# An attention-and-MLP kernel on one core: exponential tiles in any free cells, four more VectorE units in each of two late quads, another start, value fills in quarters

## The chip, the core and the metric

The kernel runs on one core of one Trainium2 chip. The metric is the device time of one execution in microseconds (us). Executions of one kernel mostly agree within 0.3%. With one core there is no second die to compare with, so every run here counts as an ordinary (fast) one.

Two lengths have to be kept apart. The *time* is what the device reports for the execution. The *span* is what the trace shows, from the first to the last instruction.

A ratio of two kernels is the mean time of one kernel's fast runs over the mean of the other's in the same rounds. It is therefore not quite the ratio of the medians that are quoted beside it. The interval behind a ratio is a 95% interval. "Same" means within 2%.

## The reference

Attention over 32 heads and a bilinear MLP read the same `x`; a sigmoid gate mixes them. S = 2048, D = 512, a head has 16 columns, F = 1376; all inputs are bf16.

```
g = sigmoid((x * gate_w).sum(-1, keepdims=True))
q, k, v = split_heads(x @ wqkv)                  # 32 heads of 16
p = softmax(q @ k^T * 16**-0.5)                  # 32 x 2048 x 2048
a = concat_heads(p @ v) @ wo
b = ((x @ w_gate) * (x @ w_up)) @ w_down
out = g * a + (1 - g) * b
```

The softmax needs 32 x 2048 x 2048 exponentials, 134 million. As 128 x 512 tiles these are 2048 tiles. Everything in this kernel is arranged around them.

## The kernel before

The work is cut into 32 *quads*: 4 heads (index `j`) times 512 queries. A quad has 16 key tiles `kt` times 4 heads, so 64 score tiles. For each `kt`, three of the four go to ScalarE, which takes two or three neighbouring tiles in one exponential. The fourth goes to VectorE as a *unit*: a first conversion of the scores to int16 gives the bits of an approximate exponential, and three copies with shifted bits (`k` = 1, 2, 3), made for two tiles at a time by VectorE or GpSimd, refine it. The products with the values then weight the four variants by values that were scaled beforehand (`VD`, and `VE` for extra units). So ScalarE has 48 tiles in a quad and VectorE 16.

The results live in *cells*: 512 columns of bf16 in the buffer `PT` (54 cells) and, as long as or as soon as they are idle, in buffers of other data (`wv`, `hT`, `wd`). A cell is free again when the products that read it are done. All other work of TensorE (projections of q, k, v, the MLP, the output projection) is cut into *fills*, packs of matmuls that are slipped in between scores and products.

The order of instructions is not written down. A *builder* (Python in the kernel file that runs when the program is built) plays through the execution with its own estimates of durations and puts each instruction at the first place where it sees its inputs ready. The positions of the fills carry a fixed pseudo-random jitter, chosen by `SEED`. A small edit can therefore move thousands of instructions.

The parts that the change touches (cuts marked with `...`). First the constants, the first loads, the choice of units:

```
NMAIN = 54                       # cells in PT
RA = 24
HB = []                          # head groups with extra VectorE units: none
XU = {0: 2, 5: 3, 10: 0, 15: 1}
...
d_wq[0] = load("act", wq[:, :, 0:128], wcol(0, 128), ...)
d_wk[0] = load("act", wk[:, :, 0:128], wcol(D, D + 128), ...)
d_wv[0] = load("act", wv[:, :, 0:256], wcol(2 * D, 2 * D + 256), ...)
...                              # then 12 transposing loads of x on "sp"
def xd(m, kt, j):                # is this tile an extra unit of VectorE?
    return (m % NQ) // 2 in HB and XU.get(kt) == j
```

The search for free cells: `alloc` gives ScalarE the first cell of `n` consecutive free cells from one set of areas, and VectorE and GpSimd an aligned pair from another set.

```
segs = [(0, RA, 9999), (C_V, 4, 9999), (C_H, FT, EH), (C_D, 5, ED)]     # ScalarE
prs = [(RA, NMAIN, 9999), (C_D + 5, C_D + FT, ED)]                      # pairs

def alloc(n, t, pair=False, keep=0):
    if pair:
        for i in sorted(pair_starts(), reverse=True):
            if is_free(i, t) and is_free(i + 1, t):
                ...
                return i
        return None
    ...                          # tightest run of at least n free cells in a row
    return None if best is None else best[1]
```

The evacuation of the first keys, the value fill in two packs of 16 matmuls, and the copies of the first transposed x:

```
def evac(bk, last):                                    # in f_k, the keys
    if b == ch == 0:
        ev_k[b, ch] = add("act", [last], lambda a: a.activation(dst, bk.ap, ACT.Copy), ...)
        return
...
for t2 in range(2):                                    # in f_v, the values
    def mk(bk, t=t, t2=t2):
        for kt in range(KD):                           # KD = 4
            for q in range(4):
                r = e.matmul(bk.ap[...], xT[:, kt, ...], wv[:, kt, ...], ...)
    packs.append((mk, 0.5, "c"))
...
ex = now("dve", [o_last], lambda v: v.tensor_copy(xT[:, kt, 0:512], src), 0.42)
```

The exponential itself, and a pair copy on VectorE:

```
c = alloc(n, t)
k = _Task("act", [sc] + old,
    lambda a: a.activation(cell_ap(c, n), src, ACT.Exp, scale=LN2 / 128.0), ...)
...
fn = lambda v: v.tensor_single_scalar(cell_ap(c, n, I16), cell_ap(pr["cell"], n, I16), 32.0 * k, ALU.add)
```

The softmax here doesn't subtract the row's maximum and nothing guards it: scores larger than these inputs give would overflow.

## Time and profile before

| | before |
|---|---|
| time, median of 3 runs | 721.21 us (721.11 to 721.33) |
| span of the profiled execution | 719.0 us |
| ScalarE, TensorE, VectorE, GpSimd busy | 98%, 95%, 88%, 57% |
| first exponential starts | 9.43 us |
| exponentials (with the gate's small ones) | 698.8 us |
| visible waits of ScalarE among them | 1.9 us |
| last exponential to the end of the span (tail) | 8.9 us |

The last four rows add up to the span. They are read from the records of ScalarE: the third is the end of the last exponential, less the start of the first, less the waits.

The head of the profile page and the chain of waits of the kernel before. The first line has, for each engine, its busy time, its share of the span and its instructions (PE is TensorE, PEld its weight loads, DVE VectorE, ACT ScalarE, POOL GpSimd). The second has the share of each engine in the chain of work that ended last, followed back from the end:

```profile
...
PE 686.3 (95%) x9079; PEld 188.6 (26%) x9079; DVE 633.8 (88%) x1209; ACT 702.8 (98%) x688; POOL 411.6 (57%) x433
...
ACT 95%; PE 3%; DMA 1%; DVE 1%; ACTq 0%; issue 0%; DVEq 0%
...
```

95% of the chain is ScalarE. The table of windows agrees: below, after the stretch, come its length and then the busy time of each engine in it, with the instructions in brackets, the TensorE clock that was granted, and the DMA share.

```profile
...
core 0: us, PE busy (x) PEld busy (x) DVE busy (x) ACT busy (x) POOL busy (x), PEclk, DMA share, GB/s
...
100.00:200.00 100.00, 95.84 (x1268) 25.80 (x1265) 91.40 (x175) 100.00 (x98) 61.88 (x66) 1.00 0.10 29
...
600.00:700.00 100.00, 95.77 (x1240) 25.37 (x1241) 88.91 (x169) 100.00 (x97) 53.26 (x51) 1.00 0.05 15
...
```

ScalarE is busy 100.00 of 100.00 us in both stretches, and so in the others between. TensorE and VectorE stand at 89 to 96. Such a "100%" has to be read with care. The groups of exponentials by form give the mean recorded duration as the last number before the second bar:

```profile
...
L1598 ACT ACTIVATE PT<-psS 128x1024 bf16<-128x1024 f32 x326 | 359.7, 1269 | 0.0
L1598 ACT ACTIVATE PT<-psS 128x1536 bf16<-128x1536 f32 x147 | 247.4, 1695 | 0.0
...
```

An exponential of two tiles is recorded with 1269 ns, but in a steady stretch the next one *starts* 0.917 us after it (median; three tiles: 1.343 us). So neighbours overlap by about 0.35 us, and a wait shorter than that does not show. What is visible is the list of waits of ScalarE (line, what released it: us in total, times, longest):

```profile
...
ACT KE L572 <- PE psS L543: 3.9, 1, 3.9
ACT L363 <- issue: 2.9, 1, 2.9
ACT hT L1598 <- PE psS L477: 2.4, 4, 1.0
ACT oraw L1808 <- PE psS L543: 1.7, 1, 1.7
```

The two lines that read `KE` and `L363` are before the first exponential, `oraw` is after the last one. In between only the line `hT L1598` remains: four waits, 2.4 us, for scores. One of them (0.49 us) is the wait for the very first scores; the other three come to 1.91 us, and all lie before 28 us. Two of them are long: 0.67 us at 15.3 us and 1.02 us at 26.5 us. The timeline before the second one (start, duration, engine, line, operation; in brackets the idle time before it):

```profile
...
24.75 0.37 PE L477 MATMUL psS<-QM,KE 32*128 32x512 bf16 x2
...
25.06 0.83 PE L543 MATMUL psS<-xT,wk 128*32 128x512 bf16 x12
...
25.71 1.05 PE L627 MATMUL psS<-wv,xT 128*32 128x256 bf16 x32
...
26.59 0.61 PE L627 MATMUL psX<-wv,xT 128*32 128x256 bf16 x16
...
27.13 0.39 PE L477 MATMUL psS<-QM,KE 32*128 32x512 bf16 x2
...
27.56 1.02 ACT L1598 ACTIVATE hT<-psS 128x1024 bf16<-128x1024 f32 x1 [1.02 <-PE psS L477]
...
```

The last scores before the wait began at 24.75 us; then TensorE did 12 matmuls of keys, 32 and 16 of values, and only at 27.13 us the next scores.

And the way to the first exponential:

```profile
...
1.80 0.53 ACTq L316 DMA_DIRECT2D wk<-in_A_wqkv_dram  x1
...
7.24 1.05 PE L543 MATMUL psS<-xT,wk 128*32 128x512 bf16 x16 [0.38 <-DMA wk<-in_A_wqkv_dram]
8.34 0.60 ACT L572 ACTIVATE KE<-psS 128x512 bf16<-128x512 f32 x1 [3.93 <-PE psS L543]
...
9.00 0.39 PE L477 MATMUL psS<-QM,KE 32*128 32x512 bf16 x3
...
9.43 3.28 ACT L1598 ACTIVATE hT<-psS 128x1024 bf16<-128x1024 f32 x3 [0.49 <-PE psS L477]
...
```

The first key weights are issued at 1.80 us as the third load on the ScalarE queue (after half of the first x and the query weights) and land at 7.20 us, the key matmuls wait for them until 7.24 us, the copy of the keys takes 0.60 us, and the first exponential starts at 9.43 us.

### The profile page before, as it was taken

Reading aid. Unit: us, or ns where it says so; the run is one execution under the profiler, and the core shown is the slowest. Engines: PE = TensorE matmul, PEld = TensorE weight load, DVE = VectorE, ACT = ScalarE, POOL = GpSimd, SP = SyncE. Lnnn points to the kernel's source line nnn. Section 1 sums busy time; section 2 is a strip of 40 time slices with the busy share of each in tenths; the row PEclk is TensorE's granted clock in tenths of the full one; section 3 lists DMA queues with packets and bytes.
Section 4 is the critical chain, followed back from the end, with each engine's and each line's share of the span. In section 5 each row is a group of like instructions: output and inputs, shape, how many; then the busy total and the mean of one; then the engine's idle time right before and its main releaser. Section 6 shows DMA issues by size and latency. Waiting matters only on the chain.

```text
span 719.0 us, 21551 instructions
## 1 busy us (share of the span) xinstructions
PE 686.3 (95%) x9079; PEld 188.6 (26%) x9079; DVE 633.8 (88%) x1209; ACT 702.8 (98%) x688; POOL 411.6 (57%) x433
## 2 busy tenths in 40 slices
PE   8999999999999999999999999999999999999996
PEld 3323232222222222222222222222222222222222
DVE  5888999998998889889998888989888999898887
ACT  5999999999999999999999999999999999999996
POOL 3777756665665455565455564665555655555541
PEclk9999999999999999999999999999999999999999
DMA  7800001000300000100000011000000010000001
GB/s 140 255 4 32 6 17 21 18 16 8 96 21 16 18 16 19 39 18 21 17 18 12 17 34 34 17 6 17 21 17 16 14 36 24 17 16 21 10 13 46
DMA packets 33054, 21.66 MB, mean 30 GB/s; under 512 B 20380, under 2 KB 27964, under 8 KB 32960
## 3 DMA queue, kind: packets, MB, share of 16 engines
q1 hardware_dynamic: 31104, 19.51, 9.4%
q8 instruction: 72, 1.18, 0.7%
q10 hardware_dynamic: 1856, 0.79, 0.5%
q14 instruction: 22, 0.18, 0.1%
HBM read 15.12 MB, written 2.36 MB: 24 GB/s over the span
## 4 chain that ended last, share of the span: by engine, by line
ACT 95%; PE 3%; DMA 1%; DVE 1%; ACTq 0%; issue 0%; DVEq 0%
ACT PT L1598 69%; ACT wv L1598 16%; ACT hT L1598 5%; ACT wd L1598 4%; PE psS L543 1%; DMA wk<-in_A_wqkv_dram 1%; PE psO L1150 1%; PE psS L477 0%; PE psS L627 0%; PE psX L627 0%; DVE wk L851 0%; PE psX L477 0%; DVE wd L1029 0%; PE psX L543 0%; ACTq L316 0%
## 5 line engine op out<-in xcount | busy, mean ns | idle before, releaser
L1598 ACT ACTIVATE PT<-psS 128x1024 bf16<-128x1024 f32 (+1 forms) x473 | 540.0, 1402 | 0.0
L1088 POOL TENSOR_SCALAR PT<-PT 128x1024 int16<-128x1024 int16 x312 | 322.2, 1043 | 250.8 <-DVE PT L1085 129.2
L1029 DVE TENSOR_SCALAR PT<-psS 128x512 int16<-128x512 f32 x441 | 300.0, 686 | 47.4 <-PE psS L477 40.6
L477 PE MATMUL psS<-QM,KE 32*128 32x512 bf16 x1981 | 263.5, 375 | 22.7 <-ACT PT L1598 8.6
L1150 PE MATMUL psO<-PT,VS 128*18 128x512 bf16 x1597 | 220.9, 381 | 0.3 <-DVE oraw L1179 0.2
L1150 PE MATMUL psO<-PT,VD 128*18 128x512 bf16 x1400 | 204.5, 381 | 0.2
L1085 DVE TENSOR_SCALAR PT<-PT 128x1024 int16<-128x1024 int16 x380 | 155.8, 450 | 4.6 <-PE psO L1150 1.4
L1598 ACT ACTIVATE wv<-psS 128x1024 bf16<-128x1024 f32 (+1 forms) x120 | 154.7, 1335 | 0.0
L971 PEld LDWEIGHTS <-KE 32*128 32x128 bf16 x2048 | 63.1, 90 | 274.7 <-issue 273.4
L1150 PEld LDWEIGHTS psO<-PT,VS 128*18 128x18 bf16 x1597 | 51.5, 88 | 63.8 <-issue 38.1
L1150 PE MATMUL psO<-wv,VS 128*18 128x512 bf16 x257 | 63.1, 381 | 0.1
L1150 PEld LDWEIGHTS psO<-PT,VD 128*18 128x18 bf16 x1400 | 47.5, 88 | 42.1 <-issue 27.4
L543 PE MATMUL psX<-wd,hT 128*32 128x512 bf16 (+1 forms) x704 | 55.9, 385 | 0.0
L543 PE MATMUL psX<-xT,wu 128*32 128x512 bf16 x688 | 55.8, 384 | 0.0
L1598 ACT ACTIVATE hT<-psS 128x1024 bf16<-128x1024 f32 (+1 forms) x49 | 53.4, 1274 | 2.4 <-PE psS L477 2.4
L543 PE MATMUL psX<-xT,wg 128*32 128x512 bf16 x688 | 55.2, 384 | 0.0
L1029 DVE TENSOR_SCALAR PT<-psX 128x512 int16<-128x512 f32 x63 | 43.4, 688 | 8.6 <-PE psS L477 8.2
L1598 ACT ACTIVATE wd<-psS 128x1024 bf16<-128x1024 f32 (+1 forms) x34 | 42.5, 1340 | 0.0
L1088 POOL TENSOR_SCALAR wd<-PT 128x1024 int16<-128x1024 int16 x26 | 27.0, 1043 | 9.3 <-DVE wd L1085 4.2
L790 DVE TENSOR_TENSOR hT<-psX,usb 128x512 bf16<-128x512 f32 (+1 forms) x44 | 30.0, 683 | 2.1 <-PE psX L543 1.9
L758 DVE CAST usb<-psX 128x512 bf16<-128x512 f32 (+1 forms) x44 | 30.0, 681 | 2.0 <-PE psO L1150 0.9
L1211 POOL TENSOR_TENSOR OT<-oraw,rb 128x512 bf16<-128x512 f32 x16 | 20.4, 1273 | 13.7 <-DVE PT L1085 13.7
(94 smaller groups left out, 453.9 us busy)
## 6 DMA issues: line engine op xcount, KB each, us to landing
rb<-rscr SPq DMA_DIRECT2D x31, 256.0 KB
out_dram<-ost SPq DMA_DIRECT2D x12, 128.0 KB, 1.7
wu<-in_B_w_up_dram SPq DMA_DIRECT2D x1, 1376.0 KB, 8.0
wg<-in_B_w_gate_dram SPq DMA_DIRECT2D x1, 1376.0 KB, 11.6
wd<-in_B_w_down_dram SPq DMA_DIRECT2D x1, 1280.0 KB, 6.2
OT<-OX SPq DMA_DIRECT2D x60, 16.0 KB, 1.8
wo<-in_A_wo_dram SPq DMA_DIRECT2D x1, 512.0 KB, 12.3
out_dram<-wk SPq DMA_DIRECT2D x4, 128.0 KB, 1.7
```

What stands on the lines that cost most here:

```text
L477: return e.add_instruction(mybir.InstMatmult(name=nc.get_next_instruction_name(), engine=mybir.EngineType.PE, ins=[e.lower_ap(rhs), e.lowe ...
L543: return e.matmul(out_ap[32 * q : 32 * q + w, :], lhs[:, 32 * q : 32 * q + w], rhs, start=s0, stop=s1, tile_position=(0, 32 * q), skip_gro ...
L758: lambda v: v.tensor_copy(usb[0:w, n % 2, :], bk.ap[0:w, :]),
L790: lambda v: v.tensor_tensor(hT[0:w, f, :], bk.ap[0:w, :], usb[0:w, n % 2, :], ALU.mult),
L971: r = e.ldweights(w, tile_position=pos)
L1029: lambda v: v.tensor_scalar(cell_ap(pr["cell"] + i, 1, mybir.dt.int16), bk.ap, CB, 0.0, ALU.add, ALU.max),
L1085: fn = lambda v: v.tensor_single_scalar(cell_ap(c, n, I16), cell_ap(pr["cell"], n, I16), 32.0 * k, ALU.add)
L1088: fn = lambda g: g.tensor_scalar(cell_ap(c, n, I16), cell_ap(pr["cell"], n, I16), 32.0 * k, 1.0, ALU.add, ALU.mult)
L1150: r = e.matmul(psO[32 * j : 32 * j + VW, :], pv_stationary(m, kt, j, k), cell_ap(cell, 1), start=s0, stop=s1, tile_position=(0, 32 * j), s ...
L1211: lambda e: e.tensor_tensor(dst, oraw[:, s, :], rb[:, s, :], ALU.mult),
L1598: lambda a: a.activation(cell_ap(c, n), src, ACT.Exp, scale=LN2 / 128.0),
```

## The change

Its intent, in the words of the change: exponential tiles may lie in any free cells, by strided writes; VectorE takes more units in two late quads; a shorter way to the first scores; value fills in quarters. The diff is 650 lines; this is its core.

```diff
-    HB = []
-    XU = {0: 2, 5: 3, 10: 0, 15: 1}
+    HBQ = [24, 30]                       # quads with extra units
+    HB = sorted({(m % NQ) // 2 for m in HBQ})
+    XU = {1: 3, 4: 2, 7: 1, 10: 0}
...
-            return (m % NQ) // 2 in HB and XU.get(kt) == j
+            return m in HBQ and XU.get(kt) == j
```
```diff
-        d_wk[0] = load("act", wk[:, :, 0:128], wcol(D, D + 128), "dwk0", 0.5, 3.6)
+        d_wk[0] = load("sp", wk[:, :, 0:128], wcol(D, D + 128), "dwk0", 0.5, 4.4)
...
-                    ev_k[b, ch] = add("act", ..., a.activation(dst, bk.ap, ACT.Copy), ...)
+                    ev_k[0, 0, 0] = add("act", ..., a.activation(dst[:, 0:128], bk.ap[:, 0:128], ACT.Copy), ...)
+                    ev_k[b, ch] = add("act", ..., a.activation(dst[:, 128:512], bk.ap[:, 128:512], ACT.Copy), ...)
...
-            ex = now("dve", ..., v.tensor_copy(xT[:, kt, 0:512], src), 0.42)
+            if kt % 2:
+                ex = now("act", ..., a.activation(xT[:, kt, 0:512], src, ACT.Copy), ...)
+            else:
+                ex = now("dve", ..., v.tensor_copy(xT[:, kt, 0:512], src), 0.35)
```
```diff
-        def cell_ap(c, n, dt=None):
+        def cell_ap(c, dt=None):             # c: a tuple of cells
...
+            dims = [[1, 512]]
+            if len(c) > 1:
+                d = c[1] - c[0]
+                dims = [[1, 512 * len(c)]] if d == 1 else [[512 * d, len(c)], [1, 512]]
...
-        segs = [(0, RA, 9999), (C_V, 4, 9999), (C_H, FT, EH), (C_D, 5, ED)]
-        prs = [(RA, NMAIN, 9999), (C_D + 5, C_D + FT, ED)]
+        groups = [(C_H, FT, EH), (C_D, FT, ED), (C_V, 4, 9999), (0, NMAIN, 9999)]
...
+            for f in fr:                     # the free cells of one buffer
...                                           # n in a row, if there are,
+                if n == 2:
+                    return (f[0], f[1])      # else any two,
...                                           # or three or four with equal steps
```
```diff
-                def mk(bk, t=t, t2=t2):
-                        for kt in range(KD):
+                for kh in range(2):
+                    def mk(bk, t=t, t2=t2, kh=kh):
+                            for kt in (2 * kh, 2 * kh + 1):
...
-                packs.append((mk, 0.5, "c"))
+                    packs.append((mk, 0.23, "c"))
...
-        SEED = 2
+        SEED = 3
```

The cuts hold changes of bookkeeping: fills of the two quads are spread thinner, a VectorE copy may take two pairs at once, the builder's estimates of durations are adjusted, the order of the first fills is written differently.

What the built programs show: ScalarE goes from 1536 tiles in 676 exponentials (490 of two tiles, 185 of three, one of one) to 1528 tiles in 674 (494 of two, of which 12 are strided, and 180 of three, of which 2 are strided). VectorE goes from 512 to 520 first conversions. The copies of pairs stay at 424 instructions on VectorE (19 with a strided output, 2 of four tiles) and go from 344 to 354 on GpSimd (9 with a strided output). So strides are rare: 14 of 674 exponentials. Before, ScalarE looked for cells in one set of areas and VectorE and GpSimd in another; now all three may take any free cell.

## The prediction

> **What bounds the kernel now.** ScalarE. The table of windows has it always busy from 100 to 700 us. The chain of waits is 95% ScalarE, nearly all exponentials. The list of waits gives it only 2.4 us of waiting for scores (four times, all before 28 us). The span is 719.0 us; the time 721.21 us.
>
> From the ScalarE timeline, start to start, an exponential of two tiles (1024 columns) takes 0.917 us, one of three (1536) 1.343 us: 0.426 us a tile and 0.064 us an instruction. The Trainium skill, page "ScalarE: Activation LUTs", section "What ACT_TABLE_LOAD costs", says one element per cycle and lane at 1.2 GHz, 0.833 ns a column; the trace agrees (0.832). Its fixed part less overlap, 93 ns, exceeds the 64 seen; I use the trace.
>
> The span is: head 9.43 us (start of the first exponential), 698.3 us of exponentials plus 0.46 for the gate, 1.9 us of later score starvation, and a tail of 8.9 us (710.1 to 719.0).
>
> **What the change does**
>
> 1. VectorE takes 4 more units in each of quads 24 and 30. ScalarE goes from 1536 tiles in 676 instructions (490 of two, 185 of three, one of one) to 1528 in 674 (494 and 180), read from the built programs. Estimate: 4×0.917 − 5×1.343 − 0.49 = −3.5 us, all critical. VectorE gets 8 first conversions (0.69 us each recorded) and there are 12 more pair copies, of which GpSimd (57% busy) takes 10. VectorE is about 89% busy, but gets fewer projection fills in those quads; I expect it to fit.
> 2. Free cells with strides. 14 exponentials, 19 VectorE and 9 GpSimd copies become strided. Each inner run stays 512 contiguous elements, so I expect contiguous durations. ScalarE never waited visibly for a cell: direct gain nil; it supports step 1.
> 3. Shorter head. The first key weights were issued at 1.80 us and arrived at 7.20, the last wait before the first keys. They now go on the sync queue ahead of the transposing loads; I estimate arrival about 1 us earlier. Two of four x copies go to ScalarE (idle then), and the key copy (0.60 us) is split so that 128 columns (about 0.3 us) release the first scores. First exponential at about 8.5 us: −0.9 us, critical. No extra table load: a copy ran there before with one load.
> 4. Value fills in quarters let scores slip in between (a 16-matmul half takes 0.62 us of TensorE). Of 1.9 us starvation about 1.0 should remain: −0.9 us.
> 5. Tail unchanged, 8.9 us ± 0.4.
>
> Sum −5.3 us. I take back 0.5 us for new short waits of ScalarE, as everything is reordered: −4.8 us.
>
> **Prediction: 716.4 us, 8 in 10 between 714.0 and 719.0.** Chances: faster by over 2% 0.01, within 2% 0.975, slower by over 2% 0.015.
>
> **What would show it.** Step 1: exponentials 3.5 us less in total, start-to-start times still 0.917 and 1.343, no ScalarE waiting late. Step 2: strided forms with the mean of contiguous ones. Step 3: first exponential near 8.5 us. Step 4: ScalarE waiting for scores about 1 us after the first exponential. Step 5: last exponential to end 8.9 us.
>
> **What would make it wrong.** VectorE or TensorE (95% busy) cannot keep up in quads 24 and 30, so ScalarE waits there; strided writes slow ScalarE; the early key weights delay the x transposes, so later keys and values come late and early starvation grows; the last product waits for copies, lengthening the tail.

## The result and the profile after

| | time, median | runs |
|---|---|---|
| before | 721.24 us | 721.11 to 721.33, n = 4 |
| after | 715.65 us | 714.12 to 715.74, n = 4 |

The ratio is 0.9918 [0.9901, 0.9935]: 0.8% faster, "same" by the 2% rule. The profiled execution is the 714.12 us one; its span is 712.5 us. The head of its page and its chain:

```profile
...
PE 683.8 (96%) x9103; PEld 187.7 (26%) x9103; DVE 641.4 (90%) x1215; ACT 700.3 (98%) x689; POOL 428.4 (60%) x467
...
ACT 65%; PE 28%; DVE 4%; issue 2%; POOL 0%; DVEq 0%; ACTq 0%
...
```

The chain is now 65% ScalarE and 28% TensorE, where it was 95% ScalarE. It would be wrong to read this as a change of the bound. The windows and the waits, which decide it, say the opposite:

```profile
...
100.00:200.00 100.00, 95.53 (x1301) 26.68 (x1297) 93.39 (x175) 99.90 (x97) 66.10 (x74) 1.00 0.11 30
...
600.00:700.00 100.00, 96.62 (x1236) 24.74 (x1228) 91.70 (x177) 100.00 (x100) 58.06 (x56) 1.00 0.05 16
...
```

```profile
...
ACT L365 <- issue: 2.4, 1, 2.4
ACT oraw L1870 <- PE psS L551: 1.7, 1, 1.7
ACT KE L581 <- PE psS L551: 1.5, 1, 1.5
ACT xT L1774 <- PE psS L1764: 1.3, 1, 1.3
```

ScalarE is busy 99.90 and 100.00 of 100.00 us, and its list has four lines which are all before the first exponential or (`oraw`) after the last: no wait of any length worth a line remains among the exponentials. A likely reason for the new shares of the chain, argued and not tested: when ScalarE's next input and its own previous instruction are ready at nearly the same moment, the chain may go either way, and TensorE (96% busy) runs close to ScalarE.

The exponentials by form:

```profile
...
L1656 ACT ACTIVATE PT<-psS 128x1024 bf16<-128x1024 f32 x397 | 420.9, 1259 | 0.2
L1656 ACT ACTIVATE PT<-psS 128x1536 bf16<-128x1536 f32 x172 | 284.8, 1679 | 0.0
...
```

There are more lines with `PT` and fewer with other buffers, because cells are now searched in another order. The means (1259 and 1679 ns) are not longer. Start to start, an exponential of two tiles takes 0.916 us (0.917 before), one of three 1.331 us (1.343). Of the 12 strided ones of two tiles nine take 0.904 or 0.905 us, the others 0.913, 0.927 and 0.990 us; 0.904 is also the commonest value of contiguous ones, whose longest is 1.065 us.

The way to the first exponential:

```profile
...
1.27 0.45 SPq L318 DMA_DIRECT2D wk<-in_A_wqkv_dram  x1
...
6.65 1.05 PE L551 MATMUL psS<-xT,wk 128*32 128x512 bf16 x16
...
7.75 0.28 ACT L581 ACTIVATE KE<-psS 128x128 bf16<-128x128 f32 x1 [1.51 <-PE psS L551]
7.92 0.48 ACT L584 ACTIVATE KE<-psS 128x384 bf16<-128x384 f32 x1
...
8.08 0.39 PE L484 MATMUL psS<-QM,KE 32*128 32x512 bf16 x2
...
8.51 2.85 ACT L1656 ACTIVATE hT<-psS 128x1024 bf16<-128x1024 f32 x3
...
```

The key weights are issued at 1.27 us and land at 5.19 us, the key matmuls start at 6.65 us and no longer wait for them, the first copy of the keys takes 0.28 us, and the first exponential starts at 8.51 us.

The longest stretch between the starts of two groups of scores, from 8 to 32 us, is 1.41 us; before, it was 2.38 us, with 2.17 us as the next. One of the stretches after:

```profile
...
12.44 0.39 PE L484 MATMUL psS<-QM,KE 32*128 32x512 bf16 x2
...
12.75 0.84 PE L640 MATMUL psS<-wv,xT 128*32 128x256 bf16 x24
...
13.42 0.39 PE L640 MATMUL psX<-wv,xT 128*32 128x256 bf16 x8
...
13.74 0.39 PE L484 MATMUL psS<-QM,KE 32*128 32x512 bf16 x2
...
```

32 matmuls of values still go in one piece (24 and 8), just like the 32 at 25.71 us in the kernel before. What is gone is a piece of 60.

The sums of both traces side by side, with the changed kernel's second profile (the run after_again below), which caught one of its slower executions:

| us | before | after | after, second profile |
|---|---|---|---|
| time of the profiled execution | 721.61 | 714.12 | 715.66 |
| first exponential starts | 9.43 | 8.51 | 9.21 |
| exponentials | 698.76 | 695.06 | 695.36 |
| visible waits of ScalarE | 1.91 | 0.15 | 0.68 |
| tail | 8.88 | 8.83 | 8.83 |
| span | 718.97 | 712.54 | 714.08 |
| time less span | 2.64 | 1.58 | 1.58 |

So 6.43 us of span went between the first two columns: 3.70 from the exponentials, 1.76 from waits, 0.92 from the head, 0.05 from the tail. Between the first and the third column 4.89 us went: 3.40, 1.23, 0.22 and 0.05.

### The profile page after: what moved, and what is told of

Its sections match the earlier page's. It is cut to its first block, busy times and chain, and to the rows that moved or that the text cites. A ratio compares the mean times of both kernels' runs of the same rounds, so it can differ in the third digit from the quotient of the medians.

```text
span 712.5 us, 21747 instructions
## 1 busy us (share of the span) xinstructions
PE 683.8 (96%) x9103; PEld 187.7 (26%) x9103; DVE 641.4 (90%) x1215; ACT 700.3 (98%) x689; POOL 428.4 (60%) x467
## 4 chain that ended last, share of the span: by engine, by line
ACT 65%; PE 28%; DVE 4%; issue 2%; POOL 0%; DVEq 0%; ACTq 0%
ACT PT L1656 54%; PE psS L484 10%; PE psO L1190 8%; PE psX L551 8%; ACT wd L1656 4%; ACT wv L1656 4%; ACT hT L1656 2%; DVE PT L1048 1%; PE psS L551 1%; DVE PT L1125 0%; PE psX L640 0%; PE psO L1753 0%; DVE QM L616 0%; PE psX L484 0%; POOL wv L1128 0%
## 5 line engine op out<-in xcount | busy, mean ns | idle before, releaser
L1656 ACT ACTIVATE PT<-psS 128x1024 bf16<-128x1024 f32 (+1 forms) x569 | 617.9, 1386 | 0.2
L1128 POOL TENSOR_SCALAR PT<-PT 128x1024 int16<-128x1024 int16 x214 | 222.2, 1046 | 183.7 <-DVE PT L1125 99.4
L1048 DVE TENSOR_SCALAR PT<-psS 128x512 int16<-128x512 f32 x334 | 226.4, 686 | 29.0 <-PE psS L484 26.6
L1125 DVE TENSOR_SCALAR PT<-PT 128x1024 int16<-128x1024 int16 (+1 forms) x240 | 102.7, 458 | 2.6 <-PE psO L1190 0.8
L1656 ACT ACTIVATE wv<-psS 128x1024 bf16<-128x1024 f32 (+1 forms) x45 | 56.4, 1262 | 0.0
L1128 POOL TENSOR_SCALAR PT<-wv 128x1024 int16<-128x1024 int16 x43 | 44.6, 1046 | 18.2 <-DVE PT L1125 8.9
L1128 POOL TENSOR_SCALAR wv<-PT 128x1024 int16<-128x1024 int16 x36 | 37.7, 1046 | 20.2 <-PE psS L484 6.1
L1048 DVE TENSOR_SCALAR wv<-psS 128x512 int16<-128x512 f32 x68 | 46.0, 686 | 3.3 <-PE psS L484 2.9
L1190 PE MATMUL psO<-wv,VD 128*18 128x512 bf16 x208 | 46.4, 381 | 0.4 <-POOL PT L1128 0.3
L1190 PE MATMUL psO<-wv,VS 128*18 128x512 bf16 x163 | 44.7, 381 | 0.0
```

The source lines that it names most:

```text
L1048: lambda v: v.tensor_scalar(cell_ap(pr["cell"][i : i + 1], mybir.dt.int16), bk.ap, CB, 0.0, ALU.add, ALU.max),
L1125: fn = lambda v: v.tensor_single_scalar(cell_ap(c, I16), cell_ap(src, I16), 32.0 * k, ALU.add)
L1128: fn = lambda g: g.tensor_scalar(cell_ap(c, I16), cell_ap(src, I16), 32.0 * k, 1.0, ALU.add, ALU.mult)
L1190: r = e.matmul(psO[32 * j : 32 * j + VW, :], pv_stationary(m, kt, j, k), cell_ap((cell,)), start=s0, stop=s1, tile_position=(0, 32 * j), s ...
L1656: lambda a: a.activation(cell_ap(c), src, ACT.Exp, scale=LN2 / 128.0),
```

## The experiments

Twelve runs were made (two of them are the changed kernel itself); the kernels ran beside the kernel before. All gave correct results. Every row of this table comes from one run's records; "time" is the median of its runs, the other columns are of its profiled execution.

| kernel | tiles, exp. | first exp. | exponentials | waits | tail | span | time | ratio to before |
|---|---|---|---|---|---|---|---|---|
| after_again | 1528, 674 | 9.21 | 695.36 | 0.68 | 8.83 | 714.08 | 714.82 | 0.9914 [0.9901, 0.9928] |
| no_units | 1536, 670 | 8.46 | 698.30 | 0.39 | 9.08 | 716.23 | 717.81 | 0.9964 [0.9951, 0.9976] |
| no_head | 1528, 676 | 9.01 | 695.12 | 0.33 | 9.99 | 714.46 | 716.33 | 0.9935 [0.9921, 0.9948] |
| halves | 1528, 675 | 8.54 | 696.27 | 3.56 | 12.18 | 720.55 | 723.07 | 1.0026 [1.0013, 1.0038] |
| halves_reseeded | 1528, 667 | 8.46 | 696.02 | 3.90 | 9.52 | 717.90 | 719.05 | 0.9961 [0.9947, 0.9975] |
| after_reseeded | 1528, 682 | 8.95 | 696.10 | 2.59 | 13.17 | 720.81 | 723.19 | 1.0027 [1.0009, 1.0046] |
| contig_no_units | 1536, 676 | 8.55 | 699.01 | 3.44 | 9.60 | 720.61 | 722.17 | 1.0006 [0.9991, 1.0021] |
| contig_units | 1535, 699 | 8.56 | 701.67 | 23.91 | 9.12 | 743.25 | 743.47 | 1.0294 [1.0272, 1.0316] |
| after_third | 1528, 674 | 8.78 | 695.14 | 0.14 | 8.82 | 712.89 | 715.58 | 0.9913 [0.9899, 0.9926] |
| three_quads | 1524, 680 | 8.62 | 693.72 | 0.14 | 12.77 | 715.24 | 717.29 | 0.9939 [0.9926, 0.9953] |
| quads_24_28 | 1528, 675 | 8.93 | 695.25 | 0.05 | 9.46 | 713.69 | 715.68 | 0.9918 [0.9904, 0.9931] |
| jitter_8 | 1528, 674 | 8.67 | 695.14 | 0.22 | 9.05 | 713.10 | 714.83 | 0.9906 [0.9893, 0.9920] |

The kernel before had medians of 721.19 (after_again to halves), 721.35 (halves_reseeded to contig_units) and 721.62 us (the last four).

One warning belongs in front. The builder lays out a whole new program for each edit, so a kernel "with one part undone" is also another layout. The run after_reseeded measures how much that alone can do.

### after_again: the changed kernel, unedited

> The changed kernel itself, as the yardstick of this call. Both theories: about 715.7 us, 0.992 of the time before. Of its four earlier runs three took 715.7 us at a mean granted clock of 0.997 and one took 714.1 us at 0.999. If the difference lies in when TensorE's clock rises in the head, these runs should fall into the same two groups, 1.6 us apart, and a profile of the slow group should show the first exponential about 1.5 us later than 8.51 us and everything after it unchanged. If it is ordinary scatter, the times will be spread between and not go with the clock.

Measured: 714.82 us (715.66, 714.32, 714.12, 715.33), ratio 0.9914 [0.9901, 0.9928]. The result repeats. The profile fell on the 715.66 us execution, and so it shows what a slower execution has that the quicker one of the first profile has not. Its first exponential starts at 9.21 us instead of 8.51 (0.70 us later, where the expectation had 1.5), and, against the expectation, one new wait of ScalarE appears among the exponentials:

```profile
...
ACT wv L1656 <- PE psS L484: 0.5, 1, 0.5
```

The wait is at 523 us. The windows around it, cut at the edges of the record of the granted clock:

```profile
...
518.86:522.27 3.41, 2.10 (x28) 0.60 (x28) 3.41 (x7) 3.41 (x4) 2.54 (x3) 1.00 0.00 0
522.27:525.68 3.41, 3.41 (x34) 0.48 (x26) 2.46 (x5) 2.93 (x4) 1.25 (x2) 0.50 0.02 2
...
```

In the first window TensorE was busy for 2.10 of 3.41 us. In the next it was granted half its clock (0.50), was busy all the time and could not keep up: ScalarE stands at 2.93 of 3.41. The same part of the program in the first profile, again cut at edges of that record:

```profile
...
516.47:519.88 3.41, 2.79 (x37) 0.79 (x32) 3.38 (x7) 3.41 (x5) 1.45 (x3) 1.00 0.02 5
519.88:523.29 3.41, 2.53 (x32) 0.60 (x29) 3.41 (x7) 3.41 (x5) 2.32 (x3) 1.00 0.02 2
...
```

There the two windows held 2.79 and 2.53 us of TensorE work, and the clock stayed at 1.00.

In a third profile of the same program (after_third) the window from 517.70 us held 2.32 us, and the clock stayed at 1.00 too.

What follows: in these three profiles, where windows of 3.41 us happen to cut the program goes with whether a half-clock window comes. Busy time alone does not decide it: in other kernels windows with as little (1.95 us from 699.01 us in after_reseeded) were followed by full clock. Of the 13 runs of the changed kernel in all, five took 714.09 to 714.47 us (mean granted clock 0.999 to 1.0), seven 715.58 to 715.98 us (0.997 to 0.998), one 715.33 us (0.999). Of the seven only one was profiled, so that the others have the same window is likely and not shown. The two profiles differ by 1.54 us in span: 0.70 of it head, 0.53 waits, 0.30 exponentials. Why the head differs is told under no_head.

### no_units: everything but the units

```diff
-    HBQ = [24, 30]
+    HBQ = []
```

> The changed kernel without the extra VectorE units (empty list of quads). The schedule gives ScalarE 1536 tiles in 670 instructions (472 of two, 197 of three, 1 of one) against 1528 in 674. Theory ScalarE sum: slower than the changed kernel by 17 x 1.338 + 0.49 - 22 x 0.918 = 3.0 us, about 718.7 us, head and tail unchanged, no new ScalarE waiting. Rival (the gain comes from the free choice of cells and the new order, the units only move work to a VectorE that is 90% busy): within 1 us of the changed kernel.

Measured: 717.81 us (717.66 to 719.42), ratio 0.9964. Against the changed kernel's first profile the span is 3.69 us longer: 3.24 from the exponentials, 0.24 from waits, 0.25 from the tail, and the head gives back 0.05. By the medians the kernel is 3.0 us slower than the changed one, as expected. Two of the five runs took 719.42 us at a clock of 0.997, so this kernel seems to have two groups of times too.

What follows: the units are worth about 3.2 us of exponentials and 3.7 us of span, with the tail and waits hardly touched. The size follows from the count: with the units ScalarE has 8 tiles fewer but four instructions *more*, since no_units gets by with 670 exponentials for its 1536 tiles (197 of them of three). An estimate from the start-to-start times of before: the tiles save 8 x 0.426 = 3.4 us and the instructions cost 4 x 0.064 = 0.3 us, which leaves 3.1 us; 3.24 us were measured. The remaining 2.7 us of span between this kernel and the kernel before (718.97 less 716.23) come without any unit.

### no_head: the old start in the changed kernel

```diff
-        d_wk[0] = load("sp", wk[:, :, 0:128], wcol(D, D + 128), "dwk0", 0.5, 4.4)
+        d_wk[0] = load("act", wk[:, :, 0:128], wcol(D, D + 128), "dwk0", 0.5, 3.6)
...      # one copy of all 512 columns of the first keys, as before
-            if kt % 2:
+            if False:
```

> The changed kernel with the three head edits undone (first key weights on the ScalarE queue, one key copy, all four x copies on VectorE); 1528 tiles in 676 instructions. Theory: first exponential at about 9.4 us instead of 8.5, so 0.9 us slower plus 0.1 us for the two instructions: about 716.7 us; nothing made up later, since ScalarE is never idle afterwards. Rival: the later start is absorbed because scores and cells wait anyway: within 0.3 us of the changed kernel.

Measured: 716.33 us (716.24 to 716.36), ratio 0.9935. The first exponential starts at 9.01 us. The span is 1.92 us longer than the changed kernel's first profile: head 0.50, waits 0.18, tail 1.16, exponentials 0.06.

The kept traces show where the head's time goes. In no_head the key matmuls wait for the key weights, as in the kernel before:

```profile
...
6.83 0.55 PEld L551 LDWEIGHTS psS<-xT,wk 128*32 128x32 bf16 x16 [0.32 <-DMA wk<-in_A_wqkv_dram]
...
9.01 1.02 ACT L1652 ACTIVATE hT<-psS 128x1024 bf16<-128x1024 f32 x1 [0.49 <-PE psS L484]
...
```

Both old starts issue these weights at 1.80 us, but they landed at 7.20 us in the profile of before and at 6.79 us in that of no_head. The first exponential follows 2.2 us later in both (9.43 and 9.01). So the 0.42 us between the two old starts is the landing of one load, and not an edit. With the new start the key weights land by 5.38 us in every profile and hold nothing up.

Two other things then set the head. All 14 profiles begin at half clock and reach full clock at different moments, 4.04 to 6.86 us. In the seven profiles of the new start that had full clock by 5.1 us (4.47 in after, 4.74 in no_units, 4.04 in jitter_8), the first exponential starts at 8.46 to 8.67 us, each time 2.85 or 2.86 us after the query weights land (5.60 to 5.82 us), so that landing is the likely limit. Where full clock came later, this distance grows: 2.93 us with full clock at 5.33 (contig_no_units), 2.95 at 5.71 (after_third), 3.30 at 6.07 (quads_24_28), 3.41 at 6.10 (after_reseeded), 3.53 at 6.86 us (after_again, where the query weights land at 5.68 us, against 5.66 in after).

What follows: against no_head the edits of the head are worth 0.50 us: the key matmuls start 0.18 us earlier (6.65 against 6.83) and the first copy of the keys is 0.32 us shorter (0.28 against 0.60). Against the kernel before they are worth 0.92 us, with 0.59 us in place of the 0.18, because there the load landed later. These are single executions of the old start; how often the load is that late is not shown. The tail of 9.99 us can hardly come from edits of the first 9 us; it is most likely a matter of layout, and at 1.16 us it is more than the edits themselves are worth. The two times of this call alone (716.33 less 714.82, so 1.5 us) would have tripled their value. The expectation of a first exponential at 9.4 us was missed, by that landing.

### halves and halves_reseeded: values again in packs of 16 matmuls

```diff
-                for kh in range(2):
+                for kh in range(1):
-                            for kt in (2 * kh, 2 * kh + 1):
+                            for kt in range(KD):
-                    packs.append((mk, 0.23, "c"))
+                    packs.append((mk, 0.46, "c"))
```

halves_reseeded has `SEED = 6` as well, for another layout of the same thing.

> The changed kernel with value fills in two packs of 16 matmuls instead of four of 8; 1528 tiles in 675 instructions. Theory: the early starvation of ScalarE comes back in part: 0.15 us of waiting after the first exponential becomes 0.8 to 1.8 us, the time rises by the same 0.7 to 1.6 us. Rival (the order of the first fills removed the starvation, not their size): waiting stays under 0.4 us and the time within 0.4 us.

> The changed kernel with value fills in halves again, but with another value (6 for 3) of the jitter that shuffles the positions of the fills, so that the builder lays out another order. 1528 tiles in 667 instructions (473 of two, 194 of three): by the durations read, 693.8 us against 694.3 of the changed kernel. Theory (in the first halves run most of the 8 us came from an unlucky layout, not from the size of the fills): only the early starvation stays, 1 to 2 us of ScalarE waiting before 30 us, tail near 9 us, time 715 to 717 us. Rival (halves themselves cost 8 us): about 723 us again, with waits spread up to 130 us and a tail of about 12 us.

Measured: 723.07 us (ratio 1.0026) and 719.05 us (ratio 0.9961). The first is far outside both of its expectations, the second between its two. Taken by their times alone they would say that quarters are worth 3.5 to 8 us. The traces say otherwise. The longest wait of ScalarE among the exponentials is 1.44 us in halves and 1.46 us in halves_reseeded, at about 22 us in both. In the list of waits of halves_reseeded from 9 to 60 us:

```profile
...
ACT PT L1656 <- PE psS L484: 1.7, 2, 1.5
PE psX L551 <- DMA xT<-in_A_x_dram: 1.6, 1, 1.6
...
```

TensorE stood 1.6 us at a key fill, in order, for the fourth chunk of x, which a transposing load had not yet landed; halves has the same wait. The stretch between scores there is 3.1 us. This is a fill placed too early by the builder. Five profiles with quarters have that wait of TensorE too, but shorter (0.23 to 1.07 us). Whether larger packs lead the builder to place the fill earlier is not tested. Apart from it, the longest stretch between the starts of scores from 8 to 32 us was 1.30 us in halves and 1.33 us in halves_reseeded, so no longer than with quarters (1.41 us), and only a wait of 0.27 us at 14 us in each is new there. The rest of halves' 723.07 us is mostly its tail (12.18 us), 1.2 us more exponentials and 1.5 us of waits at 49, 89 and 115 us.

What follows: that packs of 16 value matmuls by themselves make long stretches without scores is not borne out. ScalarE's waits before 30 us are nevertheless longer in both (1.72 and 1.74 us, of the size that the theory foretold) than in any of the profiles with quarters (0.05 to 0.89 us), though by another way, the chunk of x. What the size is worth stays open: these two runs do not part it from the place that the builder gives the fills.

### after_reseeded: the changed kernel with another jitter

```diff
-        SEED = 3
+        SEED = 5
```

> The changed kernel with nothing altered but the jitter value (5 for 3). 1528 tiles in 682 instructions (518 of two, 164 of three): 695.0 us of exponentials by the durations read, 0.7 us more. Theory (layout luck is as large as the parts of the change): 3 to 10 us slower than the changed kernel, with ScalarE waits in the middle of the run and a tail of over 11 us in which VectorE copies and the last products lag behind the last exponential. Rival (the parts decide, the layout does not matter): within 1.5 us of the changed kernel.

Measured: 723.19 us (722.39 to 725.32), ratio 1.0027: 7.5 us slower than the same kernel with jitter 3, and no better than the kernel before. The exponentials took 696.10 us, 1.0 us more; the waits 2.59 us, 2.4 us more; the tail 13.17 us, 4.3 us more.

What follows: the jitter, which computes nothing, moves the time by more than the whole change. The figure for the exponentials moves by 1 us, the waits and the tail by much more. So single runs here can be trusted for the sum of the exponentials to about 1 us, and the tail and the waits have to be read from each trace and not booked on an edit.

### contig_no_units and contig_units: cells in a row only

Both have the old search for free cells in the changed kernel (in a row for ScalarE, aligned pairs for copies, no copies of four tiles). With it come back the separate areas for ScalarE and for the pairs, and the old test for enough free cells. So these runs undo the free search as a whole, and the strides are only one part of it. contig_no_units has no units either; contig_units has them, and `SEED = 0`.

```diff
-        groups = [(C_H, FT, EH), (C_D, FT, ED), (C_V, 4, 9999), (0, NMAIN, 9999)]
+        segs = [(0, RA, 9999), (C_V, 4, 9999), (C_H, FT, EH), (C_D, 5, ED)]
+        prs = [(RA, NMAIN, 9999), (C_D + 5, C_D + FT, ED)]
...      # alloc and the test for enough free cells as in the kernel before
-        M4 = 1
+        M4 = 0
```

> The changed kernel without the extra units and with the old allocation, consecutive cells only (no strided writes). 1536 tiles in 676 instructions (492 of two, 184 of three): 697.8 us by the durations read, against 697.4 for the same without units with free cells. Theory: without the extra units consecutive cells nearly suffice; 0.4 to 3 us slower than the run without units, so 718 to 721 us, with a few us of ScalarE waiting for cells at most. Rival (strided cells alone were the gain): over 721 us, as slow as before or slower.

> The changed kernel with the extra units kept, but consecutive cells only (jitter value 0, the best of those built). The builder could keep only one of the eight units on VectorE (1535 tiles on ScalarE) and mostly two-tile instructions (560 of two, 138 of three, 1 of one, 699 in all): 699.2 us by the durations read. Theory (free cells are what makes the extra units possible): ScalarE waits 15 us or more in all where no run of cells is free, time 730 to 745 us. Rival (the units fit without strides): below 719 us.

Measured without units: 722.17 us, ratio 1.0006, so back at the kernel before. Against no_units the span is 4.38 us longer: 3.05 of it waits of ScalarE, 0.71 exponentials, 0.52 tail and 0.09 head. Its waits, 3.44 us in all, have three places: 0.84 us at 21 us, when TensorE waited 1.1 us for a chunk of x; 1.71 us at 157 us, when a key fill was not begun before 156.39 us and the scores needed its keys; and 0.84 us at 634 to 638 us, in a window of half clock. None of them is a wait for a cell. By its time this run meets the rival of its expectation (over 721 us); by its waits it doesn't show that the search was the gain.

Measured with units: 743.47 us, ratio 1.0294. The waits of ScalarE, longest first:

```profile
...
ACT PT L1657 <- PE psO L1190: 17.8, 5, 7.6
ACT wd L1657 <- PE psO L1190: 2.4, 2, 1.9
...
```

These waits, 20.2 us, end with products (`psO`), and products are what frees cells: ScalarE had scores and no cells to write to. (The last scores before the longest wait, which ends at 128.26 us, were issued at 122.73 us.) Parts of the two longest waits lie in windows of half clock, 124.55 to 127.96 and 148.44 to 155.27 us, so slow products are in their length too. With the lesser waits it is 23.9 us. Besides, the builder gave seven of the eight units back to ScalarE, which has 1535 tiles in 699 exponentials, 23 more than with the free search.

What follows: strides are used by only 14 of 674 exponentials and save no time in any of them, yet with the old search the units did not work in the layout that ran. Whether the strides do that, or that ScalarE and the pairs may now share all cells, was not tested apart. The prediction had step 2 as a support of the units, with nothing of its own. That the free search as a whole supports them is borne out: 20 us of waits for cells are far outside what a change of layout did in after_reseeded (2.59 us of waits in all). That the search does something without them is not shown: the 4.38 us of contig_no_units are of the kind and size that a layout makes. Each of the two is one layout only.

### after_third: the changed kernel beside the last three

> The changed kernel once more, as the yardstick of this call on its chip. Expected: 714.1 us in runs where TensorE reaches full clock early and no window in mid-run falls to half clock, up to 715.7 us where one or both go the other way.

Measured: 715.58 us (714.09 to 715.98), ratio 0.9913 [0.9899, 0.9926]. The third measurement of the same program agrees with the first two.

### three_quads: a third quad with extra units

```diff
-    HBQ = [24, 30]
+    HBQ = [17, 24, 28]
```

> Extra VectorE units in three quads (17, 24 and 28) instead of two; 1524 tiles in 680 instructions (516 of two, 164 of three): 693.1 us of exponentials by the durations read, 1.2 us less than with two quads. Theory (VectorE, at 90%, has no room for more: it passes the debt to the end): the last exponential ends about 1 us earlier or not at all, but the copies of the last units lag, the tail grows from 8.8 to 11 us or more, and the time is 715.5 to 718.5 us. Rival (ScalarE alone bounds the kernel, every unit moved pays 0.4 us): tail 8.8 us, time about 1.2 us under the changed kernel.

Measured: 717.29 us (717.11 to 717.35), ratio 0.9939: slower than the changed kernel beside it (after_third) by 1.7 us. The exponentials took 693.72 us, 1.42 us less than with two quads (1524 tiles, in 680 exponentials). All of that and more came back at the end: the tail is 12.77 us, 3.95 us longer. ScalarE's wait after its last exponential was 1.7 us in the changed kernel; here it is

```profile
...
ACT oraw L1870 <- PE psS L551: 4.4, 1, 4.4
...
```

and TensorE, at that time, works on what is left over after the last product:

```profile
...
703.72 0.39 PE L1190 MATMUL psO<-wv,VD 128*18 128x512 bf16 x2
703.93 0.61 PE L551 MATMUL psX<-wd,hT 128*32 128x512 bf16 x8
704.36 1.47 PE L551 MATMUL psS<-wo,OT 128*32 128x512 bf16 x24
705.66 0.60 PE L551 MATMUL psX<-wd,hT 128*32 128x512 bf16 x8
706.09 0.23 PE L551 MATMUL psS<-usb,sel 128*32 128x128 bf16 x4
...
```

Packs of the down projection (`wd,hT`), of the output projection (`wo,OT`) and the last denominators take turns. In the changed kernel's first profile only output projections and denominators are left there; the down projections were done during the exponentials.

What follows: what ScalarE gained came back at the end. A likely way, argued and not shown by a run of its own: in quads with extra units VectorE has less room to evacuate fills, the fills move later, and with a third quad some moved past the last exponential. It is one layout, so that a third quad could never pay is not shown either.

### quads_24_28: two other quads

```diff
-    HBQ = [24, 30]
+    HBQ = [24, 28]
...
-        SEED = 3
+        SEED = 0
```

> A candidate to beat both kernels: extra units in quads 24 and 28 (the last quads but one are left alone), jitter value 0. 1528 tiles in 675 instructions (495 of two, 179 of three, 1 of one): 694.4 us of exponentials, as in the changed kernel. Theory: the same sum, so within 1 us of the changed kernel, either way by waits and tail alone; the tail near 8.5 us. Rival: leaving quad 30 alone frees VectorE at the end and takes over 1.5 us off the tail.

Measured: 715.68 us (715.04 to 716.35), ratio 0.9918 [0.9904, 0.9931]. The exponentials (695.25) and the waits (0.05) are those of the change, the tail is 0.6 us longer. Between these two choices of quads the time shows no difference.

### jitter_8: the changed kernel with a third jitter

```diff
-        SEED = 3
+        SEED = 8
```

> A second candidate: the changed kernel with jitter value 8 for 3, nothing else. 1528 tiles in 674 instructions, the same forms as the changed kernel: 694.3 us of exponentials. Theory: within 1 us of the changed kernel. Rival (the layout with value 3 was a lucky one): 2 us slower or more.

Measured: 714.83 us (714.68 to 715.14), ratio 0.9906 [0.9893, 0.9920], in all four runs at a clock of 1.0. The changed kernel beside it had 0.9913 [0.9899, 0.9926] with its two groups at 714.1 to 714.5 and 715.6 to 716.0 us. The intervals overlap: that this version beats the changed kernel is not resolved. It is the steadier one in these four runs.

## Why the prediction was right, and where it was not

The time was predicted as 716.4 us, between 714.0 and 719.0; it was 715.65 us. The time was right to 0.75 us. Point by point:

- **The bound** was right. ScalarE is at 100% in the windows of both kernels, and what was gained is nearly all time of ScalarE.
- **Step 1, the units: -3.5 us, right.** The exponentials took 3.70 us less in the first pair of profiles, 3.40 in the second; no_units gives 3.24. VectorE went from 88% to 90% busy and did not fall behind.
- **Step 2, strides: right.** Strided exponentials start 0.904 us apart in the median, contiguous ones 0.916. "It supports step 1" is true of the free search as a whole: with the units and without it, ScalarE waited 20.2 us for cells in contig_units. How much of that the strides do is not shown, nor a gain of their own.
- **Step 3, the head: the start right, one part off.** 8.51 us against a predicted 8.5 us. The split copy gave 0.32 us, about as predicted. The key weights landed 2.01 us earlier (5.19 against 7.20), where about 1 us was estimated; only 0.59 us of it could be used, since the query matmuls come first on TensorE. The prediction took one landing of the old load as fixed: in no_head it came 0.41 us sooner, and there the edits are worth 0.50 us. Nor had it considered that the moment of full clock moves the head: in a slower execution of the same program the first exponential starts at 9.21 us.
- **Step 4, starvation: mis-sized, and its cause is open.** Of 1.91 us, 0.15 us remained, where 1.0 us was predicted. The waits went down by 1.76 us in the first profile and by 1.23 us in the second, where one wait from a half-clock window came in. With packs of 16 the stretches without scores did not become longer (halves, halves_reseeded), so quarters are not shown to be the cause in the way that the prediction had in mind; the waits before 30 us did grow there, at a chunk of x.
- **The take-back of +0.5 us** for new waits: hardly any late waits in the two quick executions that were profiled (0.10 and 0.09 us after 30 us); 0.5 us, at a half-clock window, in the slower one. The prediction named the amount and not the cause.
- **Step 5, the tail: right** (8.83 against 8.9 us). It was not as safe as the 0.4 us margin suggested: other layouts of the same kernel have 9.05 and 13.17 us.
- **What lies outside the span** was silently kept at the 2.2 us of before. The median span of the four runs after is 714.05 us, and 719.0 less the predicted 4.8 us gives 714.2 us, so the span was predicted to 0.15 us. The rest of the error is this term: time less span is 1.56 to 1.64 us in the 13 runs of the change and 1.88 to 3.38 us in 29 runs of the kernel before. So about 0.6 us of the gain lies before the first or after the last recorded instruction. The other kernels of the experiments have 1.54 to 2.33 us: halves, with the new start, 1.77 to 1.85, and no_head, with the old one, 1.75 to 1.84, so the start alone does not set it. No run here tells why; it stays open.

Three of the four runs behind the median are near the time of the slower profile, and its span fell by 4.89 us against a predicted 4.8. That is partly luck: in that profile the head gave 0.7 us less than predicted and the early starvation 1.0 us more (1.91 us went down to 0.05), and the take-back of 0.5 us met a wait that the prediction did not have in mind. The closeness of the sum is no evidence for these parts.

## What to carry to other kernels

When one engine is always busy, its sum of start-to-start times is the quantity to predict: the change in it was foreseen to 0.3 us from the durations in one trace, while waits and tail moved by microseconds with the layout alone, and the head by 0.4 to 0.7 us with the landing of one load and the moment of full clock. If a scheduler lays the program out anew at each edit, run the same kernel with another jitter before a difference between two versions is booked on an edit, and split each trace into head, busy sum, waits and tail. Freedom of placement that saves no time in any instruction can still be what lets another step work, and work that is moved off the bounding engine can come back in the tail.

## What the Trainium skill lacked or had wrong

- Page "ScalarE: Activation LUTs", section "What ACT_TABLE_LOAD costs": its 0.833 ns a column agrees with the 0.832 ns of this trace (0.426 us for 512 columns). Its fixed part, 186 ns less an overlap of about 93 ns, gives 93 ns; here the fixed part start to start is 64 ns. The overlap is larger too: records of two tiles are 1.27 us long and start 0.917 us apart, which leaves 0.35 us.
- The same section has the table load at about 1283 ns, which agrees with the 1.28 us of both traces. That copies can be put on ScalarE ahead of exponentials without another load agrees with the section "Table sets: the hidden batching unit" on that page: the change adds three copies there, and the trace still has one load.
- No page gives a time for an exponential whose output is strided in pieces of 512 columns. Here, of 12 with two tiles, nine took 0.904 or 0.905 us from start to start and the others up to 0.990 us, against 0.916 us in the median for contiguous ones; two of three tiles took 1.331 and 1.358 us against 1.331 us.
- Page "TensorE: Matmul & The Clock Gate", section "What's actually happening": its free-running window of 3413 ns agrees, for the edges of the clock record lie multiples of 3.413 us apart. Its table has the half clock come after at least one idle window. Here windows that were far from idle were followed by half clock: TensorE was busy for 2.10 of 3.41 us in after_again, 2.17 of 3.41 in halves_reseeded, 2.20 of 3.42 in contig_no_units. The profile's busy time gives no threshold: windows with less, 1.77 of 3.42 us in halves (from 18.43 us) and 1.95 of 3.41 in after_reseeded (from 699.01 us), were followed by full clock.
- The page says that the start at half clock costs under 1% and varies. Here full clock came between 4.04 and 6.86 us, and for one program the first exponential moved with it from 8.51 to 9.21 us, which is 0.1% of the time and an eighth of the whole gain.
